# Two arms of a run-time branch change places: the general attention first, the banded one second

## Chip, core and metric

The kernel runs on one core of a Trainium2 chip. The metric is the device time of one execution in microseconds (us), the median of several runs. The engines of the core are PE (matrix multiplication), DVE (vector), ACT (activation functions), POOL (general) and SP (which only issues transfers here); each has its own instruction stream, and they meet through semaphores. In the profile, PEld is PE's loading of weights, a name that ends in q (SPq, DVEq) is an engine's sequencer, and L679 is line 679 of the kernel.

## What is computed

Attention with 8 heads over 768 positions, in which a query sees the first `n_global` positions and the last `n_local` ones, then two feed-forward blocks. Cut to what matters:

```python
def _attn_ref(q, k, v, n_global, n_local):
    scores = scale * np.matmul(q, k.transpose(0, 1, 3, 2))
    rel = pos[:, None] - pos[None, :]
    keep = (pos[None, :] < n_global) | ((rel >= 0) & (rel < n_local))
    scores = np.where(keep, scores - slopes * dist, -1e9)
    a = softmax(scores)
    return np.matmul(a, v)

def reference(**kwargs):
    x = _attn_ref(...)             # 1536 tokens x 512
    h = x @ w_in                   # 512 x 2048
    x = (h * np.tanh(log1p(exp(h)))) @ w_out
    xn = x / rms(x) * rms_g
    g, val = xn @ w_gate, xn @ w_val   # 512 x 1536 each
    return (silu(g) * val) @ w_out
```

The inputs are `n_global` = 8 and `n_local` = 96, and they reach the kernel as tensors: it learns their values only while it runs.

## The kernel before

The program has three stretches. First comes common work: the two limits are loaded (L219), PE runs eleven matrix products on a tile of ones that nobody reads (L261), DVE derives from the limits one word that is 1 when a narrow band of keys is enough (`flag_i`, L285 to L288), every engine loads that word into a register (L289), and DVE alone goes on to make the maps of distances and masks (L297 to L316). Then the branch, one compare-and-branch instruction on each of the five engines (L958). Then one of two arms, each of which is a whole kernel from there on: attention and both feed-forward blocks.

`attention_banded` needs `n_local` from 1 to 97 and `n_global` up to 32. It walks over 48 units (2 batches, 4 pairs of heads, 6 tiles of 128 queries). For a unit, PE makes the scores (L653), DVE adds the bias and finds the extremes (L679), ACT takes the exponentials with their sums (L692), POOL scales (L708), PE transposes (L717), ACT copies out (L725), and PE multiplies by the values (L738). The order on each engine is written out by a small planner from a table of positions. ACT makes the first two heads' biases at the arm's start (L629). SP loads values (L603 to L606) and weights (L129) there. `attention_general` does the same over all 768 keys, for any limits. Both end in `mlps`: products of split numbers (L350, L402), and the result is added up by DVE (L414) and written out by twelve transfers on SP's queue (L557), the last three at the very end. With the inputs above the banded arm runs.

An arm ends with a jump to the common end of the program (also listed as L958). There SP waits for all transfers to have landed, and all engines meet (L1008). The instructions of the two arms lie one behind the other in each engine's stream, in the order in which the code names them.

```python
    banded = nc.values_load(flag_i[0:1, 0:1], min_val=0, max_val=1, ...)   # L289
    ...
    with tc.If(banded == 1) as c:                                          # L958
        attention_banded()
    with c.Else():
        attention_general()
```

Of the kernel before, what the change touches and what calls it, by code (L numbers as in the profile page):

```python
# [60 lines left out]
def tile_attention_mish_swiglu(  # L61
# [201 lines left out]
    for n in (3, 3, 3, 2):  # L263
# [25 lines left out]
    banded = nc.values_load(  # L289
        flag_i[0:1, 0:1],  # L290
        min_val=0,
        max_val=1,
        skip_runtime_bounds_check_because="a product of comparisons, 0 or 1",
    )
# [660 lines left out]
            convert(0, NW_EARLY)  # L955
        mlps(0)

    with tc.If(banded == 1) as c:  # L958
        attention_banded()
    with c.Else():  # L960
        attention_general()


# [48 lines left out]
```

## Time and profile before

| | us |
|---|---|
| median of 3 runs | 669.16 |
| lowest and highest | 667.61, 669.68 |
| the profiled execution | 668.87 |
| its span, first to last instruction | 667.1 |
| PE busy | 653.8 |
| DVE busy | 450.6 |
| ACT busy | 378.4 |

The profiled execution took 668.87 us, of which 1.8 us lie outside the span. PE is busy nearly all along; the arm's attention fills about the first 90 us, the feed-forward blocks the rest. Two short stretches matter for a change of the branch: the few microseconds around L958 at the start, and those between the last arithmetic and the end.

### The profile page before, as it was taken

What the parts mean: (1) busy time and instruction counts of PE and PEld (TensorE: products, weight loads), DVE (VectorE), ACT (ScalarE), POOL (GpSimd) and SP (SyncE); (2) the same over time, 40 slices, a digit from 0 to 9 for tenths busy, and PEclk for the clock granted to TensorE, in tenths of its full rate; (3) what the DMA queues carried; (4) which work ended last, traced back from release to release, by engine and by line L of the source; (5) the groups of instructions that cost most, each with busy time, mean ns of one, the idle gap of its engine ahead of it and who ended that gap; (6) DMA issues with size and microseconds to landing.
All of it is one profiled execution on the core that took longest, in us unless ns stands there. A gap on an engine that the chain in (4) does not pass through costs nothing.

```text
span 667.1 us, 9833 instructions
## 1 busy us (share of the span) xinstructions
PE 653.8 (98%) x3712; PEld 582.9 (87%) x3712; DVE 450.6 (68%) x1029; ACT 378.4 (57%) x716; POOL 68.0 (10%) x124
## 2 busy tenths in 40 slices
PE   8999999999999999999999999999999999999996
PEld 4777888899999999999888999999999999999995
DVE  7798868887787778776986887773376873222222
ACT  6999888898888888888796332321222221111111
POOL 3688810000000000001000000000000000000000
PEclk9999999999999999999999999999999999999999
DMA  8976332221131113221212222220122100011011
GB/s 251 333 243 206 116 119 96 94 65 63 64 96 63 64 64 94 64 64 64 70 57 64 64 76 83 92 67 0 32 64 95 64 1 0 1 48 38 11 48 52
DMA packets 26663, 54.19 MB, mean 81 GB/s; under 512 B 2544, under 2 KB 14576, under 8 KB 26608
## 3 DMA queue, kind: packets, MB, share of 16 engines
q1 hardware_dynamic: 26608, 53.49, 24.8%
q8 instruction: 31, 0.51, 0.3%
q14 instruction: 24, 0.20, 0.1%
HBM read 50.34 MB, written 3.15 MB: 80 GB/s over the span
## 4 chain that ended last, share of the span: by engine, by line
PE 82%; DVE 8%; ACT 5%; DMA 2%; issue 1%; SPq 0%; DVEq 0%; POOL 0%; POOLq 0%
PE mm L350 44%; PE s L402 29%; PE s L717 3%; PE s L738 3%; PE mm L653 3%; DMA v<-in_v_dram 1%; DVE x L414 1%; DVE d L379 1%; DVE bits L176 1%; ACT junk L448 1%; ACT L374 1%; ACT L370 1%; DVE bits L182 1%; DVE g L480 1%; DVE w L201 1%
## 5 line engine op out<-in xcount | busy, mean ns | idle before, releaser
L350 PE MATMUL mm<-hl,w 128*128 128x384 f32 x1920 | 349.6, 336 | 0.0
L350 PEld LDWEIGHTS mm<-hl,w 128*128 128x128 f32 x1920 | 336.7, 188 | 7.3 <-issue 0.7
L402 PE MATMUL s<-w,g 128*128 128x512 f32 x1008 | 247.6, 394 | 3.4 <-ACT g L476 2.1
L402 PEld LDWEIGHTS s<-w,g 128*128 128x128 f32 x1008 | 186.5, 188 | 42.4 <-DVE g L480 3.6
L543 ACT ACTIVATE r<-mm 128x384 f32<-128x384 f32 x48 | 23.5, 490 | 128.6 <-PE mm L350 128.5
L544 DVE TENSOR_TENSOR r<-r,mm 128x384 f32<-128x384 f32 x48 | 26.4, 549 | 65.9 <-ACT r L543 65.9
L414 DVE TENSOR_TENSOR x<-x,s 128x512 f32<-128x512 f32 x60 | 40.2, 686 | 40.3 <-PE s L402 40.2
L476 ACT ACTIVATE g<-r 128x384 fp32r<-128x384 f32 x48 | 25.2, 525 | 71.6 <-DVE r L544 71.6
L379 DVE TENSOR_TENSOR d<-d,mm 128x384 f32<-128x384 f32 x64 | 32.5, 549 | 35.3 <-ACT d L376 35.3
L708 POOL TENSOR_SCALAR e<-e,s 128x256 f32<-128x256 f32 (+1 forms) x96 | 49.3, 530 | 22.8 <-ACT e L692 9.7
L182 DVE SCALAR_TENSOR_TENSOR bits<-stage,bits 128x512 int32<-128x512 int32 x68 | 47.6, 700 | 2.1
L176 DVE SCALAR_TENSOR_TENSOR bits<-stage,bits 128x512 int32<-128x512 int32 x68 | 47.4, 698 | 2.1
L476 ACT ACTIVATE g<-d 128x384 fp32r<-128x384 f32 x64 | 33.5, 526 | 24.3 <-DVE d L379 22.8
L692 ACT ACTIVATE e<-e,s 128x256 f32<-128x256 f32 (+1 forms) x96 | 46.6, 517 | 0.1
L480 DVE TENSOR_TENSOR g<-r,g 128x384 fp32r<-128x384 f32 x48 | 26.8, 559 | 28.4 <-ACT g L476 28.4
L201 DVE TENSOR_TENSOR w<-bits,w 128x512 fp32r<-128x512 f32 x62 | 42.6, 688 | 0.0
L374 ACT ACT_TABLE_LOAD x32 | 41.1, 1283 | 0.6
L370 ACT ACT_TABLE_LOAD x31 | 39.8, 1283 | 0.6
L197 ACT ACTIVATE w<-bits 128x512 fp32r<-128x512 f32 x62 | 38.2, 616 | 0.0
L370 ACT ACTIVATE d<-mm 128x384 f32<-128x384 f32 x64 | 29.9, 491 | 11.3 <-PE mm L350 9.8
L679 DVE CUSTOM_DVE_ANT_0 e<-mm,bias 128x256 f32<-128x256 f32 (+1 forms) x96 | 33.7, 391 | 3.7 <-PE s L717 3.0
L480 DVE TENSOR_TENSOR g<-d,g 128x384 fp32r<-128x384 f32 x64 | 32.6, 551 | 0.7 <-ACT g L476 0.7
(77 smaller groups left out, 463.0 us busy)
## 6 DMA issues: line engine op xcount, KB each, us to landing
stage<-in_w_out_dram SPq DMA_DIRECT2D x28, 512.0 KB, 3.2
stage<-in_w_in_dram SPq DMA_DIRECT2D x16, 512.0 KB, 3.8
stage<-in_w_gate_dram SPq DMA_DIRECT2D x12, 512.0 KB, 3.5
stage<-in_w_val_dram SPq DMA_DIRECT2D x12, 512.0 KB, 3.4
k<-in_kT_dram SPq DMA_DIRECT2D x6, 704.0 KB, 6.0
v<-in_v_dram SPq DMA_DIRECT2D x8, 384.0 KB, 4.7
out_dram<-x SPq DMA_DIRECT2D x12, 256.0 KB, 2.1
q<-in_qT_dram SPq DMA_DIRECT2D x6, 384.0 KB, 6.8
```

The lines of the kernel that those rows point to most:

```text
L176: dve.scalar_tensor_tensor(self.bits, self.lw, 29, self.bits, op0=ALU.logical_shift_right, op1=ALU.bitwise_or,)
L182: dve.scalar_tensor_tensor(self.bits, self.hw, -1073741824, self.bits, op0=ALU.bitwise_and, op1=ALU.bitwise_or,)
L201: engine.tensor_tensor(self.wt[:, 1, :], self.fl, self.wt[:, 0, :].bitcast(F32), op=ALU.subtract)
L350: pe.matmul(ps[:, 0:BT], w[:, wi, col], xs[kc][:, xi, :], start=kc == 0 and i == 0, stop=kc == NK - 1 and i == 2,)
L370: act.activation(self.t[:, i, :], self.h[i], AF.Tanh, scale=0.5)
L374: act.preload_act_table_set("trig_and_small")
L402: pe.matmul(acc[m], gt[:, gi, tok], w[:, wi, :], start=c % 4 == 0 and i == 0, stop=c % 4 == 3 and i == 2,)
L414: dve.tensor_tensor(y, y, acc[m], op=ALU.add)
L476: act.activation(gt[:, 0, :], x, AF.Copy)
L480: dve.tensor_tensor(gt[:, 1, :], x, gt[:, 0, :].bitcast(F32), op=ALU.subtract)
L692: act.activation(e, e, AF.Exp, scale=-1.0, bias=s[:, 0, u % 2, j : j + 1], accum_out=s[:, 1, u % 2, j : j + 1],)
L708: pool.tensor_scalar(e, e, es[u // 2][1][:, 3, u % 2, j : j + 1], 0.0, op0=ALU.mult, op1=ALU.add,)
```

## The change

The condition is turned round and the two arms change places in the code. Nothing else is edited. The test still has the same result, the same arm runs, and its instructions stand in the same order on every engine with the same waits.

```diff
-    with tc.If(banded == 1) as c:
+    with tc.If(banded == 0) as c:
+        attention_general()
+    with c.Else():
         attention_banded()
-    with c.Else():
-        attention_general()
```

What changes is where the arms lie. On DVE around the branch, before (`e`, `s` and `bias` belong to the banded arm):

```order
L315 COPY x_85<-x_85 128x32
L316 TENSOR_TENSOR x_85<-x_85 128x96
L958 COMPARE_AND_BRANCH
L679 ISA e_233,s_234<-mm_180,bias 128x128
L679 ISA s_234 128x1
L679 ISA e_233,s_234<-mm_181,bias 128x128
```

And now (names with `g_` belong to the general arm):

```order
L315 COPY x_85<-x_85 128x32
L316 TENSOR_TENSOR x_85<-x_85 128x96
L958 COMPARE_AND_BRANCH
L872 TENSOR_SCALAR g_glob<-g_rel,small 128x768
L889 TENSOR_SCALAR g_drop<-g_rel,small 128x768
L890 TENSOR_SCALAR g_tmp<-g_rel 128x768
```

The first instruction of the banded arm stood directly behind the branch; now the whole general arm, 2,172 rows of this list on DVE, lies between them. On PE it is 1,473 rows, on ACT 779, on SP 98 and on POOL 23 (a row can stand for several equal instructions).

At the end of the banded arm on DVE, before, the general arm follows the jump:

```order
L414 TENSOR_TENSOR x_87<-x_87,s_864_6082 128x512
L414 TENSOR_TENSOR x_87<-x_87,s_865_6083 128x512
L414 TENSOR_TENSOR x_87<-x_87,s_866_6084 128x512
L958 UNCONDITIONAL_BRANCH
L872 TENSOR_SCALAR g_glob<-g_rel,small 128x768
L889 TENSOR_SCALAR g_drop<-g_rel,small 128x768
```

And now these are the last rows of DVE's list, with the common end directly behind them:

```order
L480 TENSOR_TENSOR g_14878<-r_14875,g_14878 128x384
L414 TENSOR_TENSOR x_87<-x_87,s_2125_14781 128x512
L414 TENSOR_TENSOR x_87<-x_87,s_2126_14782 128x512
L414 TENSOR_TENSOR x_87<-x_87,s_2127_14783 128x512
L958 UNCONDITIONAL_BRANCH
```

So the stretch of instructions to be jumped over moved from behind the banded arm to before it, on all five engines.

## Rows read from the trace of the kernel before

**Rows 1.** The page: busy time, and the chain that ended last, by engine.

```profile
PE 653.8 (98%) x3712; PEld 582.9 (87%) x3712; DVE 450.6 (68%) x1029; ACT 378.4 (57%) x716; POOL 68.0 (10%) x124
...
PE 82%; DVE 8%; ACT 5%; DMA 2%; issue 1%; SPq 0%; DVEq 0%; POOL 0%; POOLq 0%
```

**Rows 2.** Busy time by stretch: us, engines' busy time, PE clock, DMA share, GB/s.

```profile
5.00:10.00 5.00, 4.84 (x25) 2.04 (x25) 4.37 (x26) 2.56 (x11) 0.00 (x0) 1.00 0.97 319
...
8.00:20.00 12.00, 11.09 (x88) 6.95 (x86) 9.52 (x54) 11.94 (x47) 7.44 (x16) 1.00 1.06 340
20.00:40.00 20.00, 19.56 (x206) 14.74 (x202) 17.29 (x84) 20.00 (x70) 13.93 (x27) 1.00 1.00 300
40.00:60.00 20.00, 19.83 (x206) 14.67 (x204) 18.11 (x81) 19.98 (x72) 17.27 (x31) 1.00 0.76 251
60.00:72.00 12.00, 11.86 (x122) 8.73 (x118) 10.84 (x45) 12.00 (x44) 10.56 (x20) 1.00 0.42 112
```

**Rows 3.** Chain of waits, first 20 us: start, us, what.

```profile
8.54 8.37 DMA v<-in_v_dram
16.91 0.14 issue
17.05 0.44 PE s L738 x4
```

**Rows 4.** L958 up to 10 us: durations min/median/max in ns, first and last start.

```profile
L958 ACTq COMPARE_BRANCH  x1: 39/39/39, 5.4 to 5.4; - x1
L958 POOLq COMPARE_BRANCH  x1: 45/45/45, 5.4 to 5.4; - x1
L958 PEldq COMPARE_BRANCH  x1: 90/90/90, 5.4 to 5.4; - x1
L958 SPq COMPARE_BRANCH  x1: 49/49/49, 6.0 to 6.0; - x1
L958 DVEq COMPARE_BRANCH  x1: 50/50/50, 7.6 to 7.6; - x1
```

**Rows 5.** Timeline, first 20 us: start, us, engine, line, operation, idle time before it.

```profile
1.53 4.87 PE L261 MATMUL mm<-x 128*128 128x512 bf16 x11 [1.53 <-DVE small L254]
...
6.33 1.11 PE L653 MATMUL mm<-x,x 64*128 64x128 f32 x8
...
7.44 1.15 ACT L629 ACTIVATE bias<-x 128x128 bf16<-128x128 f32 x4 [5.23 <-DVE x L313]
...
7.57 0.26 DVE L316 TENSOR_TENSOR x<-x 128x96 f32<-128x96 f32 x1
7.89 0.29 DVE L679 CUSTOM_DVE_ANT_0 e<-mm,bias 128x128 f32<-128x128 f32 x1
...
8.49 0.38 ACT L692 ACTIVATE e<-e,s 128x128 f32<-128x128 f32 x1
...
9.19 0.60 PE L261 MATMUL s<-x 128*128 128x512 bf16 x2
...
17.05 0.44 PE L738 MATMUL s<-pt,v 128*64 128x128 f32 x4 [0.49 <-DMA v<-in_v_dram]
```

**Rows 6.** L958 again, from 655 us on: the jumps at the arm's end.

```profile
L958 ACTq COMPARE_BRANCH  x1: 38/38/38, 657.5 to 657.5; - x1
L958 PEldq COMPARE_BRANCH  x1: 3530/3530/3530, 658.7 to 658.7; - x1
L958 DVEq COMPARE_BRANCH  x1: 63/63/63, 661.0 to 661.0; - x1
L958 SPq COMPARE_BRANCH  x1: 42/42/42, 662.2 to 662.2; - x1
```

**Rows 7.** L1008, what each engine did first behind its jump (655 to 664.2 us).

```profile
L1008 ACTq DRAIN  x1: 80/80/80, 660.2 to 660.2; - x1
...
L1008 SPq EVENT_SEMAPHORE  x6: 17/28/28, 662.7 to 663.9; - x6
L1008 PEldq DRAIN  x1: 8/8/8, 662.4 to 662.4; - x1
L1008 DVEq DRAIN  x1: 58/58/58, 663.9 to 663.9; - x1
```

**Rows 8.** The end: last arithmetic, last transfers (issue to landing), SP's wait, SP's last steps.

```profile
659.63 2.05 DVE L414 TENSOR_TENSOR x<-x,s 128x512 f32<-128x512 f32 x3 [0.99 <-PE s L402]
660.35 1.80 SPq L557 DMA_DIRECT2D out_dram<-x  x3
...
L557 SPq DMA_DIRECT2D out_dram<-x x3: 332/382/646, 660.4 to 661.8; - x3
DMA to landing us min/median/max: 2.4/2.8/4.3
...
SPq L1008 <- DMA out_dram<-x: 3.1, 2, 2.2
...
L1008 SPq DRAIN  x3: 7/7/13, 666.2 to 666.6; - x3
```

**Rows 9.** The nine earlier transfers of L557, 580 to 645 us: issue to landing.

```profile
DMA to landing us min/median/max: 2.0/2.1/2.7
```

**Rows 10.** Instruction packets by queue, MB, share of 16 engines: 661.5:663, 664:664.9, 37:38.6.

```profile
q14 instruction: 1, 0.01, 2.1%
...
q8 instruction: 1, 0.02, 6.1%
...
q14 instruction: 1, 0.01, 5.9%
```

## Prediction

> **What bounds the kernel now.** I read the page first. PE is busy 653.8 of 667.1 us and holds 82% of the chain that ended last [rows 1], so in the long run only PE's work counts, and this change touches none of it. What it can touch is the two edges of the arm, so I looked next at the stretches. From 8 to 72 us ACT is busy 11.94 of 12, 20.00 of 20, 19.98 of 20 and 12.00 of 12 us [rows 2]: the attention goes at ACT's pace, and whatever delays ACT's first exponential moves the whole attention. That exponential starts at 8.49, right after DVE's first step of the arm at 7.89 [rows 5]. The chain of waits names another candidate in the first 17 us, the transfer of the values, which lands at 16.91 and lets PE go on at 17.05 [rows 3]. At the other edge the arithmetic is over at 661.7, but the last instruction comes 5.4 us later. In between SP waits for the last output transfer [rows 8].
>
> Then I looked at the branch itself. At the start it costs next to nothing: on DVE it is issued at 7.6 and takes 50 ns, and the first step behind it runs at 7.89 although DVE was occupied until 7.83 [rows 4, 5]. The arm that runs lies directly behind the branch. At the end every engine jumps over the general arm, and the trace shows what that costs. ACT jumps at 657.5 and does its next thing at 660.2, 2.7 us later. DVE: 661.0 to 663.9, 2.9 us. PE: 658.7 to 662.4, 3.7 us, and its own jump is recorded as 3.53 us long. SP, whose part of the general arm is short, needs 662.2 to 662.7, 0.5 us [rows 6, 7]. In those stretches the queues that carry instructions move packets again, one for example between 661.5 and 663 [rows 10]. The jump is dear where its target is far, I read, because the instructions must be fetched first.
>
> **The change part by part.** It moves no arithmetic. It makes the branch at the start a far jump, and the jump at the end a near one.
>
> *Start, added.* Each engine pays its own far jump at its own time. PE: 5.4 + 3.7 = 9.1, then its scores, of which eight take 1.11 us [rows 4 to 7]; the first are there before 9.7. ACT: 5.4 + 2.7 = 8.1, then its four bias steps, 1.15 us, done by 9.3. DVE branches last, because it makes the maps first: 7.6 + 2.9 = 10.5, and then 0.3 to its first step, as from 7.6 to 7.89 now. So DVE comes last, and its first step moves to about 10.8. ACT's first exponential moves with it, from 8.49 to 11.4, and since ACT then is never idle until 72 us, nothing gives the delay back there. After that PE and DVE take turns on the chain without waiting for a transfer, so I let the delay pass to the end. POOL's jump lies well before its first need, that is free.
>
> How sure is 2.9? From below: DVE's last step before the end jump ended at 661.7, so of the 2.9 only 2.2 are proved to be waiting for the jump. From above: the fetch at the start competes with the input transfers, whose engines are busy 0.97 of the time, while it was nearly alone at the end [rows 2]. A packet of the same kind and size took 2.1% of 16 engines over 1.5 us, 0.50 us, at the end, and 5.9% over 1.6 us, 1.51 us, in the worst loaded case that I found [rows 10]. That gives 2.9 + 1.0 = 3.9. I take 2.9, since the end jump of DVE, too, ran beside transfers (the output). **Start: +2.9, from +2.2 to +3.9.**
>
> *Start, SP.* SP branches at 6.0. If its jump is dear there, it issues the first weights and the values about 2.9 us later. That is covered: the transfers issued before the branch keep the transfer engines busy at 0.97 from 5 to 10 us [rows 2], and the values were issued long before they landed (8.37 us, [rows 3]). If the cover fails, the values land up to 2.9 us later, at 19.8; PE would want them at 17.05 + 2.9 = 19.95. So it costs nothing either way.
>
> *End, removed.* DVE, ACT and PE no longer jump far. That alone would be worth nothing: DVE's arrival at 663.9 is earlier than SP's, whose next step is at 666.2 [rows 7, 8]. SP waits for the last of three output transfers, which is issued at 661.8 and takes 4.3 us to land. The nine earlier ones took 2.0 to 2.7, 2.1 in the middle [rows 8, 9]. What is special about the last is its company: from 664.0 to 664.9 one packet of PE's instruction queue occupies a transfer engine for 6.1% of 16 engines over 0.9 us, 0.88 us [rows 10], and it comes right after PE's far jump was done at 662.4. I take it that this fetch, and the smaller ones before it, hold up the last piece of the transfer. Without them it lands 2.1 us after its issue, at 663.9 instead of 666.1: **End: -2.2.** Bounds: if it lands as late as the second of the three did (2.8 us), 664.6 and -1.5; if the lateness has another cause, 0.
>
> *Sum:* +2.9 - 2.2 = +0.7. Made against the profiled execution: 668.87 + 0.7 = 669.57. That execution lies 0.29 below the median of 669.16, so the forecast for the median is 669.9.
>
> [...]
>
> **The rivals.** A measurement of this kernel can tell about 0.3%, 2.0 us, from no change.
>
> *Rival 1, slower: one far jump is not all at the start.* A fetch at the end brought engines to code that is over after two or three instructions. At the start DVE lands in the middle of an arm and runs on; if the piece fetched ends soon after its target, DVE stops again for a second fetch, or the first is slowed by the input transfers. Place: DVE between its branch and its fourth or fifth step. Price: a second wait like the first, less what runs meanwhile, so +1 to +2.9 more, in all +1.7 to +3.6: 670.9 to 672.8. It decides when DVE's first steps are more than 3.3 us late. For it: ACT has no slack [rows 2]. Against it: the pieces are not small (one packet on their queue is 0.01 MB [rows 10]).
>
> [...]
>
> *Rival 3, slower: the end gives nothing back.* The last transfer is late because it is last, or another fetch falls there. Then +2.9 remains: 672.1.
>
> *Rival 4, faster or the same: the far jump at the start is cheap or absorbed.* Either the attention starts by the values after all, and PE's wait for them soaks up part (PE idles only 0.49 there [rows 5], so this is weak), or the branch's target is at hand early, since the comparison is known from 5.4 on and DVE branches only at 7.6. Then the end's -2.2 stands alone or with a part: 667.0 to 668.5.
>
> [...]
>
> *Rival 5: nothing is moved.* The arms could be laid out in memory in another order than listed. Against it: the costs of the jumps as they are now fit the listed order on four engines. 669.2.
>
> **How the numbers follow.** Forecast 0.55 (669.9; its own range 668.9 to 671.2). Rival 1: 0.17. Rival 2: 0.05. Rival 3: 0.08. Rival 4: 0.10. Rival 5: 0.05. Slower by over 2.0 us (above 671.2): two thirds of rival 1, nearly all of 2 and 3, and a twentieth of the forecast: 0.27. Faster by over 2.0 us (below 667.2): half of rival 4: 0.05. The rest, 0.68, is the same. The range must leave out no more than 0.2: from 668.0, which takes in the better half of rival 4's upper part, to 672.5, which takes in most of rivals 1 to 3.
>
> **What would show it.** Right: DVE's branch at 7.6 followed by its first L679 at 10.6 to 10.9; ACT's first L692 at about 11.4, and every row of the attention about 2.9 later; PE's first L653 near 9.2; the last transfer landing in 2.0 to 2.8 us, with no instruction packet beside it; less than 4 us from the last L414 to the end instead of 5.4. Wrong: a first L679 later than 11.5, or a second hole in DVE's first steps (rival 1); products of L261 at 0.44 us after 9 us (rival 2); a last landing of over 4 us (rival 3); a first L679 near 8 (rivals 4 and 5).

## The result, and the profile after

The changed kernel takes 673.87 us in the median of six runs (672.74 to 674.67), the kernel before 668.47 (667.61 to 669.68, six runs with those shown ahead). The ratio is 1.008, with an interval of [1.007, 1.0091]: slower by 5.4 us, where the forecast was +0.7 and its range ended at +3.3. The profiled execution of the changed kernel took 674.67 us, its span 672.9.

The page first: busy times, and the chain that ended last by engine, as in [rows 1].

```profile
PE 656.1 (98%) x3712; PEld 583.8 (87%) x3712; DVE 450.2 (67%) x1029; ACT 378.7 (56%) x716; POOL 68.0 (10%) x124
...
PE 84%; DVE 8%; ACT 5%; issue 2%; POOL 0%; POOLq 0%; DVEq 0%
```

No work was added; PE's 2.3 us more are the same 3712 products. "DMA 2%" has gone from the chain and "issue" has doubled from 1% to 2%: time in which an engine waited for nothing that the profile shows. The chain of waits over the first 30 us says where, in one piece, and whose:

```profile
6.21 6.77 issue
12.98 1.66 PE mm L653 x8
```

The timeline of the same stretch, beside [rows 5] (start, us, engine, line, operation, idle time before it):

```profile
10.66 1.12 ACT L629 ACTIVATE bias<-x 128x128 bf16<-128x128 f32 x4 [8.45 <-issue]
...
12.70 0.33 SPq L129 DMA_DIRECT2D stage<-in_w_in_dram  x1
...
12.98 1.66 PE L653 MATMUL mm<-x,x 64*128 64x128 f32 x8 [6.78 <-issue]
...
14.56 0.61 PE L261 MATMUL s<-x 128*128 128x512 bf16 x1
14.79 0.29 DVE L679 CUSTOM_DVE_ANT_0 e<-mm,bias 128x128 f32<-128x128 f32 x1 [6.91 <-PE mm L653]
```

The first L679 is at 14.79, not at 7.89 as before and not at 10.8 as forecast, and it was PE that it waited for. The branches themselves are issued when they were (columns as in [rows 4]), but PE's is now recorded as 7195 ns long:

```profile
L958 ACTq COMPARE_BRANCH  x1: 45/45/45, 5.4 to 5.4; - x1
L958 PEldq COMPARE_BRANCH  x1: 7195/7195/7195, 5.5 to 5.5; - x1
L958 SPq COMPARE_BRANCH  x1: 45/45/45, 6.0 to 6.0; - x1
L958 DVEq COMPARE_BRANCH  x1: 67/67/67, 7.6 to 7.6; - x1
```

From the branch to the next thing that the engine does: ACT 5.44 to 10.60, 5.2 us; PE 5.51 to 12.76, 7.25 us; SP 5.96 to 12.70, 6.7 us. DVE's 7.0 us are an upper bound, since its next thing waits for PE's scores.

Why so long shows in the DMA queues (packets, MB, share of 16 engines), first from 5.4 to 9 us, then from 9 to 11:

```profile
q1 hardware_dynamic: 567, 1.18, 93.2%
```

```profile
q1 hardware_dynamic: 96, 0.43, 52.9%
q14 instruction: 4, 0.03, 3.9%
q8 instruction: 1, 0.02, 3.0%
```

In the 3.6 us after the first branches not one instruction packet moves; the transfer engines are full of the input transfers that SP issued before the branch. The first four packets start between 9.06 and 9.76, PE's at 10.30 (PE's queue is q8; DVE's and SP's, where they jump alone below, are q14). The windows of the start, beside [rows 2] (us, busy times with counts, PE clock, DMA share, GB/s), show two more effects:

```profile
5.00:9.00 4.00, 1.20 (x4) 0.21 (x2) 2.25 (x13) 0.00 (x0) 0.00 (x0) 1.00 0.94 318
9.00:10.50 1.50, 0.00 (x0) 0.00 (x0) 0.00 (x0) 0.00 (x0) 0.00 (x0) 0.59 0.75 302
10.50:12.70 2.20, 0.00 (x0) 0.00 (x0) 0.00 (x0) 1.12 (x4) 0.00 (x0) 0.50 0.05 19
12.70:20.00 7.30, 7.02 (x28) 3.68 (x29) 3.13 (x20) 3.94 (x16) 1.52 (x4) 0.53 0.91 233
20.00:40.00 20.00, 19.86 (x198) 14.46 (x198) 16.27 (x87) 19.57 (x70) 13.48 (x29) 1.00 0.96 299
```

From 10.5 to 12.7 the transfer engines stand nearly idle (0.05), because SP itself is stuck behind its branch and issues nothing. And PE, which had stood still since 6.2, is granted a clock of 0.50 from 9.3 to 19.5, where the kernel before shows 1.00 from 8 to 20 [rows 2].

The end turned out better. The last output transfers of the changed kernel, as in [rows 8]:

```profile
L557 SPq DMA_DIRECT2D out_dram<-x x3: 332/333/333, 668.5 to 669.9; - x3
...
DMA to landing us min/median/max: 2.0/2.0/2.1
```

The last L414 is over at 669.85, and the end comes 3.03 us later instead of 5.40.

The profiled difference of 5.8 us thus splits without a rest. First L679: +6.9. From the first to the last L679, 68.0 us before and 69.1 now: +1.1. From there to the end of the last L414: +0.2. From there to the end: -2.4.

### The profile page after: what moved, and what is told of

The parts are those of the page before. It is cut to its first block, busy times and chain, and to the rows that moved or that the text cites. A ratio compares the mean times of both kernels' runs of the same rounds, so it can differ in the third digit from the quotient of the medians.

```text
span 672.9 us, 9828 instructions
## 1 busy us (share of the span) xinstructions
PE 656.1 (98%) x3712; PEld 583.8 (87%) x3712; DVE 450.2 (67%) x1029; ACT 378.7 (56%) x716; POOL 68.0 (10%) x124
## 4 chain that ended last, share of the span: by engine, by line
PE 84%; DVE 8%; ACT 5%; issue 2%; POOL 0%; POOLq 0%; DVEq 0%
PE mm L350 44%; PE s L402 28%; PE mm L653 4%; PE s L717 3%; PE s L738 3%; DVE x L414 1%; DVE d L379 1%; DVE bits L176 1%; ACT junk L448 1%; ACT L374 1%; ACT L370 1%; DVE bits L182 1%; PE mm L261 1%; DVE g L480 1%; DVE bits L167 1%
## 5 line engine op out<-in xcount | busy, mean ns | idle before, releaser
L414 DVE TENSOR_TENSOR x<-x,s 128x512 f32<-128x512 f32 x60 | 40.2, 686 | 40.3 <-PE s L402 40.2
L476 ACT ACTIVATE g<-r 128x384 fp32r<-128x384 f32 x48 | 25.2, 525 | 71.8 <-DVE r L544 71.8
L679 DVE CUSTOM_DVE_ANT_0 e<-mm,bias 128x256 f32<-128x256 f32 (+1 forms) x96 | 33.9, 391 | 10.5 <-PE mm L653 9.0
```

What stands on the lines that cost most here:

```text
L414: dve.tensor_tensor(y, y, acc[m], op=ALU.add)
L476: act.activation(gt[:, 0, :], x, AF.Copy)
```

## The experiments

The general arm never runs, so it can be replaced by anything: how long it is on one engine sets how far that engine jumps. All such kernels leave the general attention out. The times beside them are of the kernel before on the same chip. It took 667.9 to 668.65 there and 668.47 above, so a difference taken across two of these groups is uncertain by about 0.7 us.

**Distance, or merely being the second arm?** The general arm is cut to a single transfer, with the banded arm first (`e1_short_banded_first`) and second (`e2_short_general_first`).

```diff
     def attention_general():
-        fresh()
         sp.dma_start(gcol, rms_g)
-        ...
-        mlps(0)
```

> The order of before, with the general arm cut to one transfer, so that the jump at the end of the banded arm is near on every engine (the general attention is left out; with these inputs it does not run). If the far jumps' instruction fetches hold up the last output transfer: it lands 2.0 to 2.8 us after its issue instead of 4.3, and the time is 668.5 - 2.2 = 666.3. Rival, the last transfer is late for another reason: landing stays at 4.3 and the time at 668.5.

> The order of the change, with the same short general arm (general attention left out). The branch is still taken, but its target is near. If the distance, through the fetch, is what costs: DVE's first L679 near 8, PE's clock stays at 1.00, 666.3 as the run with the banded arm first. Rival, a taken branch at this place is dear in itself: first L679 near 14.8 as in the changed kernel, about 671.5 to 674.

Measured: 666.54 (ratio 0.9972 [0.9961, 0.9984]) and 666.59 (0.9975 [0.9964, 0.9986]), beside 668.25. The two orders are alike. In the second, PE's branch is recorded as 229 ns long, and SP issues its next transfer 0.17 us after its branch. Its L679 as a group (count, durations in ns, first and last start), and under it that of the changed kernel:

```profile
L679 DVE CUSTOM_DVE_ANT_0 e<-mm,bias x96: 275/419/426, 7.7 to 75.6; 128x256 f32<-128x256 f32 x80, 128x128 f32<-128x128 f32 x16
```

```profile
L679 DVE CUSTOM_DVE_ANT_0 e<-mm,bias x96: 273/417/425, 14.8 to 83.9; 128x256 f32<-128x256 f32 x80, 128x128 f32<-128x128 f32 x16
```

With the short arm the attention starts and ends as early as before the change. So a taken branch costs nothing that these times show when its target is near. Against 666.6, the far jump at the start costs 673.87 - 666.59 = 7.3 us and the far jump at the end 668.25 - 666.54 = 1.7; their difference, 5.6, is the 5.4 measured within 0.2.

**Which engine's jump?** The general arm is first, and long on one engine alone: 2,200 idle products on PE, or 2,300 fills of a small tile on DVE, or 200 small transfers on SP.

In this order (`e3_pe_long_general_first`, `e4_dve_long_general_first`, `e5_sp_long_general_first`):

```diff
     def attention_general():
-        ...
+        ps = bank("s3")
+        warm(ps, 2200, ones)
```

```diff
     def attention_general():
-        ...
+        scrap = cpool.tile([P, 8], F32, tag="scrap", name="scrap")
+        for _ in range(2300):
+            dve.memset(scrap, 0.0)
```

```diff
     def attention_general():
-        ...
+        scrap = cpool.tile([P, 2, 2], I32, tag="scrap", name="scrap")
+        for _ in range(200):
+            sp.dma_start(
+                scrap[:, 0, :],
+                n_local.bitcast(I32).rearrange("(o w) -> o w", o=1).to_broadcast((P, 2)),
+            )
```

> The order of the change; the general arm is 2,200 idle products on PE and nothing else (general attention left out), so only PE has a far jump at the start. If PE's jump sets the delay (7.3 us there in the changed kernel, and the lower clock after it): first L653 at 12 to 13, clock 0.5 for some 10 us, 673 to 674. Rival, DVE's jump sets it: about 667 to 669.

> The order of the change; the general arm is 2,300 small fills on DVE and nothing else (general attention left out), so only DVE has a far jump at the start. It shows DVE's own price, which the changed kernel hides behind its wait for PE's scores. If the fetch waits until the input transfers are through (about 10.5 us): first L679 at 11.5 to 13, clock 1.00, 666.3 + 4 to 5 = 670 to 671.5. Rival, DVE's jump alone gives the whole delay: first L679 near 14.8, 673.

> The order of the change; the general arm is 200 small transfers on SP alone (general attention left out), so only SP jumps far at the start. In the changed kernel SP's first issue behind the branch came at 12.7 us instead of 6.1, and the transfer engines stood still for about 3 us. If SP's lateness sets the delay of the whole: values land some 5 us later, 669 to 671. If, as predicted, it is covered: 666.5 to 667.5.

Measured: PE 673.33 (1.0073 [1.0055, 1.009], beside 668.25), DVE 672.20 (1.0055 [1.0037, 1.0073]), SP 671.45 (1.0041 [1.0022, 1.0059], beside 668.65). Over the 666.6 of the near jump these are +6.7, +5.6 and +4.9: each engine's jump alone costs most of the 7.3, and they overlap. SP's comes from a group in which the kernel before took 0.4 us more, so it may be 4.5; ACT's and POOL's jumps were not tried alone. The timelines of `e3_pe_long_general_first` and of `e4_dve_long_general_first` show the two ways to a late first L679: by PE's scores, and by DVE's own jump (14.21, nearer to its rival's 14.8 than to the 11.5 to 13 expected). Between them stands the L679 of PE's kernel as a group.

```profile
11.54 1.65 PE L653 MATMUL mm<-x,x 64*128 64x128 f32 x8 [6.13 <-issue]
...
13.32 0.29 DVE L679 CUSTOM_DVE_ANT_0 e<-mm,bias 128x128 f32<-128x128 f32 x1 [5.63 <-PE mm L653]
```

```profile
L679 DVE CUSTOM_DVE_ANT_0 e<-mm,bias x96: 275/416/425, 13.3 to 82.4; 128x256 f32<-128x256 f32 x80, 128x128 f32<-128x128 f32 x16
```

```profile
14.21 0.29 DVE L679 CUSTOM_DVE_ANT_0 e<-mm,bias 128x128 f32<-128x128 f32 x1 [6.64 <-issue]
```

DVE's single packet moves at 12.1 only, 4.8 us after its branch; here SP was not stuck and kept the transfer engines full:

```profile
8.00:12.00 4.00, 1.24 (x6) 0.44 (x6) 0.00 (x0) 0.33 (x2) 0.00 (x0) 1.00 1.00 349
```

With SP's jump alone the first L679 is on time, but the last one comes at 80.5, 4.9 us later than with the near jump. The window of `e5_sp_long_general_first`, then its L679, then the step of PE that waits for the values:

```profile
8.00:12.00 4.00, 3.58 (x24) 1.80 (x24) 3.58 (x23) 4.00 (x18) 1.25 (x4) 1.00 0.52 204
```

```profile
L679 DVE CUSTOM_DVE_ANT_0 e<-mm,bias x96: 274/417/425, 7.7 to 80.5; 128x256 f32<-128x256 f32 x80, 128x128 f32<-128x128 f32 x16
```

```profile
19.55 0.69 PE L738 MATMUL s<-pt,v 128*64 128x128 f32 x4 [1.04 <-DMA v<-in_v_dram]
```

SP stood still from 5.97 to 11.30, the transfer engines fell to 0.52, and the values and weights behind it came late: PE goes on with the values at 19.55 instead of 17.05 [rows 5]. A part of the 4.9 may be the clock, which in this kernel was granted at 0.50 from 18.4 to 25.2 (0.90 over 12 to 20 us, 0.87 over 20 to 40).

**Is it the queue of input transfers?** All input transfers but the first half of those for the first pair of heads move from ahead of the branch to the start of the banded arm, once with the changed order (`e9_loads_in_arm_general_first`), once with the order before (`e10_loads_in_arm_banded_first`), which shows what the move alone costs.

```diff
-    for m in range(2):
+    def first_loads(m):
         ...
-    sp.dma_start(q_first[1], qT[0, 1])
-    sp.dma_start(k_first[1], kT[0, 1])
+    first_loads(0)
     ...
     def attention_banded():
         ...
+            first_loads(1)
+            sp.dma_start(q_first[1], qT[0, 1])
+            sp.dma_start(k_first[1], kT[0, 1])
```

> The changed kernel with all input transfers but the first half of the first pair (0.5 MB) moved behind the branch. If the jumps at the start are so long because the instruction packets wait behind the input transfers: ACT and PE need 2.7 to 4 us from branch to next step instead of 5.2 and 7.3, DVE's first L679 at 10.5 to 11.5 instead of 14.8; the time 670 to 672, since the inputs themselves now come later. Rival, the length is the jump's own: PE again 7.3 us, 674 or more.

> The control: the kernel before with the same transfers moved behind the branch. The transfers are in the same order and the engines that move them were busy without a hole, so they should come 0.5 to 1.5 us later: 668.3 to 669.8.

Measured: 673.90 (1.0088 [1.0067, 1.0109]) and 671.61 (1.0053 [1.0032, 1.0073]), beside 668.65. Both are later than expected: late inputs cost 3.0 us by themselves, and the move gains nothing for the changed kernel. But between the two orders there are now only 2.3 us, and with the 1.7 of the end the jump at the start costs 4.0 instead of 7.3. The traces agree. The first L682 is at 11.39, only 3.5 us later than the 7.89 of `e10_loads_in_arm_banded_first`, where the change alone made it 6.9; from there to the last one both need 70.9. The L682 of `e10_loads_in_arm_banded_first` as a group:

```profile
L682 DVE CUSTOM_DVE_ANT_0 e<-mm,bias x96: 274/418/428, 7.9 to 78.8; 128x256 f32<-128x256 f32 x80, 128x128 f32<-128x128 f32 x16
```

The trace of `e9_loads_in_arm_general_first` (where, as in its control, the arm stands three lines lower: L656 is L653, L682 is L679), first a window, then the instruction packets from 5.4 to 8 us, then the timeline:

```profile
5.00:8.00 3.00, 0.45 (x3) 0.00 (x0) 2.25 (x13) 0.00 (x0) 0.00 (x0) 0.96 0.06 15
```

```profile
q14 instruction: 3, 0.02, 3.4%
q8 instruction: 1, 0.02, 2.4%
```

```profile
7.86 0.33 SPq L234 DMA_DIRECT2D x<-in_qT_dram  x1
...
9.59 1.66 PE L656 MATMUL mm<-x,x 64*128 64x128 f32 x8 [4.14 <-issue]
...
11.39 0.29 DVE L682 CUSTOM_DVE_ANT_0 e<-mm,bias 128x128 f32<-128x128 f32 x1 [3.60 <-PE mm L656]
```

With the transfer engines nearly idle (0.06) the packets move at 6.25 to 6.99, within 1.6 us of the branches. The jumps take 2.9 us on ACT, 3.95 on PE and 2.5 on SP: for ACT and PE the prices of the quiet end, 2.7 and 3.7 [rows 6, 7]. PE's jump can be read in three pieces. In the changed kernel its packet starts 4.8 us after the branch, moves for 1.0 and PE goes on 1.5 after that. Here: 1.6, 1.0 and 1.4. Only the wait for the start differs. It is not one number at full queues either: with PE's jump alone (`e3_pe_long_general_first`) the packet starts at 9.02, 3.7 us after the branch. And whether the queue ahead or the load of the moment sets the wait is not told apart here, since both went with the inputs.

**The clock.** Twelve more idle products ahead of the branch keep PE at work until 8.5 us.

```diff
-    for n in (3, 3, 3, 2):
+    for n in (3, 3, 3, 14):
```

> The changed kernel with 12 more idle products on PE ahead of the branch, so that PE works on while it waits for its instructions. If the lower clock from 9.3 to 19.5 us is a cost of its own beside the jump: clock 1.00 throughout, products of 512 columns at 0.3 us after the branch, and 672.4 to 672.8 instead of 673.9. Rival, the clock costs nothing because ACT sets the pace: 673.9.

Measured: 672.54 (1.0059 [1.0037, 1.0081], beside 668.65), 1.3 us under the changed kernel. Other than expected, the lower clock is not gone from its windows, but confined to 12 to 15.5 us:

```profile
5.00:12.00 7.00, 3.69 (x19) 1.56 (x19) 2.25 (x13) 1.01 (x4) 0.00 (x0) 1.00 0.77 253
12.00:15.50 3.50, 3.50 (x17) 1.81 (x15) 1.37 (x9) 1.93 (x9) 0.00 (x0) 0.51 0.65 167
15.50:20.00 4.50, 4.50 (x32) 2.61 (x32) 4.04 (x24) 3.71 (x16) 2.59 (x7) 1.00 1.11 281
```

The gain is not all the clock's, though: PE's first scores began at 11.80 instead of 12.98, because its packet started at 9.04 instead of 10.30 in this execution, and why is not settled. The clock's share is bounded by other lines. It makes the eight first scores 0.55 us longer (1.66 against 1.11 in [rows 5]), and the way from the first to the last L679 at most 1.1 us longer (69.1 against 68.0). In `e4_dve_long_general_first`, where the clock is at 0.50 from 12.5 to 19.3 (0.57 over 12 to 20 us), that way is 68.1. So the clock is worth up to 1.6 of the 7.3 us.

**The end.** The order before, with the general arm long on PE alone (`e6_pe_long_banded_first`) or on DVE alone (`e7_dve_long_banded_first`), by the same lines as above.

> The order of before; the general arm is 2,200 idle products on PE alone (general attention left out), so at the arm's end only PE jumps far. If PE's second instruction packet is what holds up the last output transfer: landing over 4 us again, 668.3. Rival, DVE's or ACT's packets hold it up: landing 2.0 to 2.8, 666.5 as with the short general arm.

> The order of before; the general arm is 2,300 fills on DVE alone (general attention left out), so at the end only DVE jumps far. If PE's packet is the cause: landing 2.0 to 2.8, DVE arrives 2.9 us after its jump and about when SP does, 666.5 to 667. Rival: landing over 4 us and 668.3.

Measured: 667.38 (0.9993 [0.9977, 1.0009]) and 668.14 (1.0011 [0.9996, 1.0027]), beside 667.9; by time alone they are not told apart, their traces are. Neither time shows the gain of the short arm (0.9972); in the profiled execution with PE alone, 0.8 us of it went in the attention (68.7 us from the first to the last L679, 67.9 with the short arm), not at the end. The last three transfers, first PE alone, then DVE alone:

```profile
L557 SPq DMA_DIRECT2D out_dram<-x x3: 332/332/332, 661.0 to 662.3; - x3
...
DMA to landing us min/median/max: 2.0/2.0/2.1
```

```profile
L557 SPq DMA_DIRECT2D out_dram<-x x3: 332/332/333, 660.1 to 661.5; - x3
...
DMA to landing us min/median/max: 2.1/3.2/3.2
```

PE alone makes its far jump of 3.66 us and fetches its two packets (at 660.2 and 664.1), and no landing is late; from the last L414 to the end it is 3.10 us, as with the short arm (3.04). DVE alone makes the second and third landing 1.1 us late, and the end comes after 4.19. DVE jumps at 660.8, right between the output transfers; its one packet of 8 KB moves at 662.28.

Two more kernels put idle products on PE at the banded arm's end, to send PE's jump to another moment.

```diff
     def attention_banded():
         ...
+        tail = bank("s3")
+        for _ in range(4):        # e11_pe_tail4; 10 in e12_pe_tail10
+            pe.matmul(tail[:, 0:P], ident, ident, start=True, stop=True)
```

> The kernel before with four idle products of 128 columns on PE at the end of the banded arm, so that PE jumps later and its second instruction packet comes after the last output has landed. If that packet is the cause of the late landing: landing 2.0 to 2.8 and 666.5 to 667. Rival: landing over 4 us as before, 668.3 or a little more.

> The same with ten idle products. PE jumps 1 to 2 us later than before; its first packet may then meet the outputs and its own arrival at the common end, 3.7 us after the jump, may become the last: 666.7 to 668. Rival as for four products: 668.3.

Measured: 667.73 (0.9999 [0.999, 1.0009]) and 668.93 (1.0014 [1.0004, 1.0023]), beside 667.9. With four products the jump hardly moved: PE's late packet lies at 663.91, as in the kernel before (664.04), yet the last transfer lands in 2.95 us instead of 4.33. With ten, PE's packet lies at 662.7 amid the output, takes 1.9 us, the last two transfers need 4.2 and 4.4, and the time is later than expected.

What the last transfer of the kernel before waited for can be looked up in its output packets (q1), first from 664.0 to 664.9 us, then from 664.9 to the end:

```profile
q1 hardware_dynamic: 1, 0.00, 0.1%
```

```profile
q1 hardware_dynamic: 1, 0.00, 0.1%
```

Each is a packet of 4 bytes, at 664.05 and at 664.91. Between them no output packet moves, and the second starts just as PE's packet (664.04, 0.88 us) ends. With four products the last output packet moves at 664.31, while PE's packet is still under way; with PE alone it moves at 664.08, just as PE's starts. So in the kernel before, 0.9 us of the late landing fit a last piece that stood behind PE's packet; the trace does not name the transfer engine, so this is read from the times. The control `e10_loads_in_arm_banded_first`, with the same far jumps at its end, has landings of 2.3 to 3.3 us and 4.11 from the last L414 to the end: the 5.40 of the kernel before was a long one.

## Why the prediction was wrong

**What bounds the kernel: right.** ACT has no slack in the attention, and a late first exponential is never made up: +6.9 at the first L679 is +8.2 at the last L414.

**The start's price per engine: the step that failed.** The prediction took the jumps of the end, 2.7 to 3.7 us, for those of the start (+2.9, at most +3.9); measured is 7.3 in time and 6.9 at the first L679. It knew that the transfer engines were at 0.97 [rows 2], but made a price of it by the packet's own duration, 0.50 against 1.51 us [rows 10]. The duration hardly changes (PE's packet 1.0 us in both `e9_loads_in_arm_general_first` and the changed kernel). What changes is the wait until it starts: 1.6 us with nothing queued, 4.8 behind the queued inputs. The durations under load tell how fast a packet moves, not how long it waits before it starts, and no row of the end, where only the small output ran, could show that. With the inputs out of the way the first L682 came at 11.39, near the 10.8 of the forecast.

**Who is last: wrong engine, by the same error.** DVE was to come last at 10.5, with PE's scores ready before 9.7. PE's scores came last, at 14.6. Both are close: DVE alone gives 14.21, PE alone 13.32. The 9.7 was also read short. In these traces the first L679 starts 0.1 to 0.2 us after the end of the eighth product, not of the first ones, and by the prediction's own rows that end was at 9.1 + 1.11 = 10.2, close to DVE's 10.5.

**SP costs nothing: its price and its cover wrong, the result nearly right.** SP's jump was reckoned at 0.5 to 2.9 us and as covered. It took 6.7 us, and the cover, transfers already queued, ran out at 10.5 us (share 0.05). When SP jumps alone, 4.9 us of the time hang on it: the values were indeed issued long before they landed, so a late issue lands late. But the prediction's second thought held in the changed kernel, where the others are as late: between 5 and 90 us the profile shows no engine that waits for a transfer, and the way from the first to the last L679 is 69.1 us, the same as with PE's jump alone, where SP is on time.

**Rival 1** (the fetch is slowed by the input transfers) had the right cause. But it placed the loss in a second hole among DVE's first steps, priced at +1 to +2.9; it was one longer hole at the branch, some 4.4 us more than the 2.9, and there was no second one.

**Rival 2** (PE's clock, given 0.05) happened, beside the rest and not instead: the granted clock was 0.50 from 9.3 to 19.5, two products of L261 at 17.11 took 1.04 us where two took 0.60 before [rows 5], and it is worth up to 1.6 us.

**The end, -2.2: right in sign and about in size, in mechanism as far as the traces go.** The changed kernel's profile gives -2.4, the timed runs 1.7: the profiled landing of 4.3 was a long one, and that the forecast from it came so near is partly luck. PE's packet and the smaller ones before it were to be the cause. PE's packet fits 0.9 us of that landing by its times, and amid the output, with ten products, landings grow to 4.4. But it does not always fall there: PE's jump alone delayed no landing, while DVE's alone, a smaller packet, made two 1.1 us late. How a packet of 8 KB does that, and why the kernel before needed 1.2 us from its last packet to the landing where the changed one needed 0.35, stays open.

**Rivals 3, 4 and 5** fell: the end did give back; the jump was neither cheap nor absent. At the start it took about 0.2 us to a near target (`e2_short_general_first`) and, on ACT, PE and SP, 2.5 to 3.95 to a far one with the input transfers out of the way (`e9_loads_in_arm_general_first`) and 5.2 to 7.25 behind them (the changed kernel).

## What to carry over

Put the arm that will run directly behind the branch, or keep the skipped code short: distance is what costs, not the branch being taken (673.87 us across the long arm, 666.59 across the short one, 666.54 with the banded arm directly behind the branch). If a far jump must be made, price it with the transfer engines as full as they will be at that moment, not by a jump elsewhere in the program (PE's took 3.7 us at the end and 7.25 at the start). And each engine tried alone pays for its own jump (PE 6.7 us, DVE 5.6, SP 4.9), the one that only issues transfers too, since behind its jump the next loads wait.

## What the runs showed of the hardware

- Instruction packets are counted on the same 16 transfer engines as the data (q14 3.9%, q8 3.0%, beside q1's 52.9%, from 9 to 11 us) and started late while those were full. At full queues the first packet started 3.6 us after the branches (5.44 to 9.06), DVE's alone 4.8 us after its own; at nearly empty ones 0.9 us (5.34 to 6.25).
- On PE the stall was recorded in the branch itself (7195 ns); on ACT, SP and DVE the branch reads 45 to 67 ns, and the stall is only seen as idle time put down to "issue" (ACT 8.45 us, 5.2 of them behind the branch; DVE, jumping alone, 6.64) or, on SP, as a gap between its issues (6.7 us from its branch).
- The length of the code jumped over on an engine did not tell SP's price: across the same general arm 0.5 us at the end and 6.7 at the start; why the end's was so cheap was not tried.
- With an instruction packet amid the output, it landed late: 3.2 us instead of 2.1 with DVE's 8 KB, 4.2 and 4.4 with PE's 16 KB among smaller ones of the other engines.
- The clock fell after PE's stall: idle from 6.2 to 12.98 us, PE was granted 0.50 from 9.3 to 19.5. With idle products until 8.5 it was 1.00 from 5 to 12 and 0.51 from 12 to 15.5.
